# Fourier tables and the local mask of a fused attention and spectral-mixing kernel: loaded by SyncE, eight partitions at a time

## The chip, the cores and the metric

The kernel runs on one core of a Trainium2 chip. The metric is the device time of one execution in microseconds (us). A core has five engines that run their own instruction streams: TensorE (PE in the profile; its weight loads are PEld), VectorE (DVE), ScalarE (ACT), GpSimd (POOL) and SyncE (SP). They wait for each other through semaphores. Transfers between the device's memory (HBM) and the core's on-chip memory (SBUF, 128 partitions) are done by 16 DMA engines. An engine's instruction stream only issues a transfer; the transfer then runs on its own. In this kernel GpSimd issues the loads of inputs and weights, SyncE and ScalarE issue small loads of constants at the start and the stores of the output at the end.

## What is computed

The input is q, k and v with 8 batches, 8 heads, 576 positions and a head dimension of 64, and the spectral weights w_r and w_i (64 modes of 512 x 512) and w_ch (512 x 512), all float32.

```python
def _attn_ref(q, k, v):
    scores = scale * np.matmul(q, k.transpose(0, 1, 3, 2))
    rel = pos[:, None] - pos[None, :]
    mask_local = (rel >= 0) & (rel < stride)                 # stride = 32
    mask_strided = (rel >= 0) & (pos[None, :] % stride == pos[:, None] % stride)
    # heads 0-3 use mask_local, heads 4-7 mask_strided
    attn = softmax(np.where(masks, scores, -1e9))
    return np.matmul(attn, v)

def _moe_ref(x, w_r, w_i, w_ch):          # x: attention's output, (8, 576, 512)
    X = np.fft.rfft(x, axis=1)            # over the positions
    # the first 64 modes are multiplied by complex 512 x 512 weights, the others dropped
    Yr = einsum(Xr, w_r) - einsum(Xi, w_i)
    Yi = einsum(Xr, w_i) + einsum(Xi, w_r)
    y = np.fft.irfft(Y, n=S, axis=1)
    u = x + y
    return u + np.maximum(u @ w_ch, 0.0)
```

## The kernel before

The kernel has three stages. First comes the attention of heads 4 to 7 (strided mask), batch by batch, with a Fourier transform of each batch's result. Then comes the attention of heads 0 to 3 (local mask), again with the transform, and between its pieces the first half of the spectral products. Last come the second half of the spectral products, the inverse transform and the output. The transforms are products with tables of sines and cosines.

Seven constants are built on the host in float16 and loaded at the start. `cFs` (128 x 2 x 6 x 64) is the Fourier table for the strided heads, `cFl` (128 x 2 x 5 x 64) for the local heads, and `cA` (128 x 704) the table of the inverse transform. `cM6` and `cM5` are the strided masks, `cMl` (128 x 256) the local mask, and `cI` the identity matrix.

```python
names = ["cFl", "cFs", "cA", "cM6", "cM5", "cMl", "cI"]
...
def const_load(eng, *which):
    for n in which:
        eng.dma_start(cs[n][:, 0 : hosts[names.index(n)].shape[1]], drams[n])
...
load_str(0, 1)                                     # GpSimd: batch 0 of v, q, k
const_load(nc.scalar, "cI", "cM6", "cM5", "cFs")
load_str(1, 1)
const_load(nc.sync, "cMl", "cFl", "cA")
load_str(2, 2)                                     # GpSimd: batches 2 and 3
w_fetch()                                          # GpSimd: the first weight tile
```

The SBUF copies of `cFs` and `cFl` hold one more row than the host's: the negated sine part, which VectorE writes while the first batch is being prepared. It stands in VectorE's program between the copies of that batch's keys.

```python
first = str_front(0)         # 10 steps: transposes of v, q and k of batch 0, with copies
for i, w in enumerate(first):
    w()
    ...
    if i == 7:               # after the first of three steps on the keys
        for n in ("cFs", "cFl"):
            nc.vector.tensor_scalar(
                out=cs[n][:, 2], in0=cs[n][:, 0], scalar1=-1.0, scalar2=None,
                op0=AluOp.mult,
            )
```

`str_front(b)` transposes the inputs of batch b on TensorE (lines 269, 285 and 324) and copies the results with VectorE and ScalarE (lines 274, 292, 260 and 330). Then the loop over the batches runs, with `str_scores` (masks at line 345, scores at 353), `str_values` (line 374) and, a batch later, the transform `dft` (line 514). The inputs pass through a ring of four slots. A load into a slot waits until TensorE has transposed what was there.

```python
for b in range(B):
    if b in (1, 3):
        load_str(b + 3, 2)                         # two batches into slots of the ring
    load_loc(*[(), (), (), (), (0,), (1, 2), (3,), (4, 5)][b])
    w_fetch([2, 1, 1, 1, 1, 1, 0, 0][b])
    front = str_front(b + 1) if b + 1 < B else loc_front(0)
    for t in range(6):
        str_scores(b, t)
        ...                                        # values, transform, parts of front
```

In the second and third stage each weight tile (two modes) is loaded into one of five buffers (three more are borrowed in the first stage), used by the products of line 547 and then filled again. `w_fetch` issues these loads on GpSimd as two transfers, real and imaginary parts. GpSimd's stream is in order: a load that waits for a buffer holds back all later ones.

Of the kernel before, what the change touches and what calls it, by code (L numbers as in the profile page):

```python
# [29 lines left out]
def _host_consts():  # L30
    s = np.arange(S)
    m = np.arange(NM)
    ang = 2.0 * np.pi * np.outer(s, m) / S
    F2 = np.stack([np.sin(ang), np.cos(ang)], axis=1)


    Fl = np.zeros((128, 2, 5, NM))
    for t in range(5):
        Fl[: SCS[t], :, t] = F2[128 * t : 128 * t + SCS[t]]
    Fs = np.zeros((128, 2, 6, NM))  # L40
    for rp in range(2):
        for j, (a, z) in enumerate(JG):
            r2 = np.arange(a, z)
            ss = (32 * np.arange(NCB)[None, :] + 2 * r2[:, None] + rp).reshape(-1)
            Fs[: len(ss), :, 3 * rp + j] = F2[ss]

    A = np.zeros((4, 2, 16, S))
    for mm in range(NM):  # L50
        e = np.zeros(S // 2 + 1, dtype=np.complex128)
        for ri, unit in enumerate((1.0, 1j)):
            e[mm] = unit
            A[mm // 16, ri, mm % 16] = np.fft.irfft(e, n=S)
    A = A.reshape(2 * NM, S)
    A[:, :512] = A[:, :512].reshape(128, 256, 2).transpose(0, 2, 1).reshape(128, 512)
    none = np.zeros((128, 64))
    A = np.concatenate([A[:, :512], none, A[:, 512:], none], axis=1)

    ms = []  # L60
    for nr in (6, 5):
        n = nr * NCB
        kc, kr = np.arange(n) // nr, np.arange(n) % nr
        qr, qc = np.arange(n) // NCB, np.arange(n) % NCB
        ok = (kr[:, None] == qr[None, :]) & (kc[:, None] <= qc[None, :])
        blk = np.zeros((128, n))
        blk[:n] = np.where(ok, 0.0, NEG)
        ms.append(blk)

    rel = np.arange(160)[None, :] - np.arange(128)[:, None]  # L70
    blk = np.where((rel >= 0) & (rel < STRIDE), 0.0, NEG)
    last = np.full((128, 96), NEG)
    last[:64, 32:] = blk[:64, :64]
    ml = np.concatenate([blk, last], axis=1)
    f16 = [a.astype(np.float16) for a in (Fl, Fs, A, ms[0], ms[1], ml)]
    return f16 + [np.eye(128, dtype=np.float16)]
# [3 lines left out]
def kernel(  # L80
# [10 lines left out]
    nc = tc.nc  # L91
# [16 lines left out]
    def psum(kind, half=False):  # L108
# [4 lines left out]
    hosts = _host_consts()  # L113
    names = ["cFl", "cFs", "cA", "cM6", "cM5", "cMl", "cI"]
    drams = {
        n: nc.inline_tensor(np.ascontiguousarray(h), name=n).ap()
        for n, h in zip(names, hosts)
    }

    more = {"cFl": 1, "cFs": 1}  # L120
    cs = {
        n: consts.tile(
            [128, h.shape[1] + more.get(n, 0), *h.shape[2:]], F16, name=n + "_s"
        )
        for n, h in zip(names, hosts)
    }

    def const_load(eng, *which):
        for n in which:
            eng.dma_start(cs[n][:, 0 : hosts[names.index(n)].shape[1]], drams[n])  # L130

    idn = cs["cI"]

# [85 lines left out]
    def load_str(b, nb):  # L219
        for vi in (2, 0, 1):  # L220
            n = 3 * (b % 4) + SLOT[vi]
            two = ring[:, n : n + 4 : 3, :]
            src = SRC[vi][b - b % 2 : b - b % 2 + 2, 4:8].rearrange(
                "b h (c r) d -> (h c) b (r d)", r=32
            )
            if nb == 2:
                nc.gpsimd.dma_start(two[0:64], src[0:64])
            else:
                nc.gpsimd.dma_start(ring[0:64, n, :], src[0:64, b % 2])
            if b % 2 == 0:  # L230
                nc.gpsimd.dma_start(two[64:72], src[64:72])
# [465 lines left out]

    psum_pools(tp=3, sc=3, av=2)
    load_str(0, 1)
    const_load(nc.scalar, "cI", "cM6", "cM5", "cFs")  # L700
    load_str(1, 1)
    const_load(nc.sync, "cMl", "cFl", "cA")
    load_str(2, 2)
    w_fetch()

# [69 lines left out]
    for b in range(B):  # L775
# [12 lines left out]
        n = 0  # L788
        nm = NMODES[b]
        for mi in range(nm):  # L790
# [3 lines left out]
            n = upto  # L794
# [46 lines left out]
    n = 0  # L841
# [4 lines left out]
    for m in range(END):  # L846
# [7 lines left out]
        n = upto  # L854
# [165 lines left out]
```

The softmax here doesn't subtract the row's maximum and nothing guards it: scores larger than these inputs give would overflow.

## Time and profile before

The median of 3 runs is 433.9 us (433.64 to 435.1). The profiled execution has a span of 434.2 us.

| | busy, us | share of the span |
|---|---|---|
| TensorE, products | 338.5 | 78% |
| TensorE, weight loads | 244.5 | 56% |
| VectorE | 215.9 | 50% |
| ScalarE | 187.5 | 43% |
| GpSimd | 129.3 | 30% |

The page cuts the span into 40 equal slices of 10.9 us. A digit is the busy share of a slice in tenths, and the lines for DMA give the busy share of the 16 engines and the rate of what they moved. The queues are listed with the number of packets, the megabytes moved and the time of their packets as a share of 16 engines' span: q0 holds GpSimd's transfers, q1 SyncE's and q10 ScalarE's. The chain of waits follows the work that ended last back to what released it. In a timeline, a line has start, duration, engine, source line, operation and operands, and in brackets the idle time before it and what ended that.

The loads of the constants have these sizes and these times from issue to landing:

| constant | issued by | KB | issued at, us | us to landing |
|---|---|---|---|---|
| cI | ScalarE | 32 | 0.74 | 2.0 |
| cM6, cM5 | ScalarE | 27 and 22.5 | 1.14 and 1.6 | 2.6 and 5.8 |
| cFs | ScalarE | 192 | 2.10 | 6.6 |
| cMl | SyncE | 64 | 0.74 | 1.8 |
| cFl | SyncE | 160 | 1.14 | 2.5 |
| cA | SyncE | 176 | 1.60 | 5.5 |

### The profile page before, as it was taken

The numbers are of one execution on the slowest core, as the hardware profiler recorded it, in microseconds if no ns is written. First come the engines' busy times: TensorE is split into PE (matmuls) and PEld (weight loads), VectorE is DVE, ScalarE is ACT, GpSimd is POOL, SyncE is SP. The second block draws the span as 40 slices with busy tenths as digits, with TensorE's granted clock in tenths as the row PEclk, the third lists the DMA queues.
The fourth block names the chain that finished last, engine by engine and source line by source line (L and its number), as shares of the span: only waits on it lengthen the run. The fifth ranks groups of instructions, "written<-read, shape, count | busy, mean of one in ns | idle before, by whom it ended". The sixth has DMA issues, their size and how long they took to land.

```text
span 434.2 us, 12103 instructions
## 1 busy us (share of the span) xinstructions
PE 338.5 (78%) x5307; PEld 244.5 (56%) x5307; DVE 215.9 (50%) x468; ACT 187.5 (43%) x352; POOL 129.3 (30%) x208
## 2 busy tenths in 40 slices
PE   1986888779985787889885566587789798968993
PEld 1865776658864575667753344454456465643441
DVE  2888678744433243342511033355436366503894
ACT  1686678634643435444440401143215123602892
POOL 6433332322332222222222222222222221200992
PEclk9999899865985859875865569887958899988999
DMA  8999999999999999999999999999999999991787
GB/s 176 210 211 213 214 212 213 211 211 213 213 212 212 214 214 212 214 214 213 214 212 213 213 214 214 212 214 215 211 214 214 212 214 214 213 182 30 272 330 261
DMA packets 29140, 92.18 MB, mean 212 GB/s; under 512 B 4064, under 2 KB 5344, under 8 KB 29088
## 3 DMA queue, kind: packets, MB, share of 16 engines
q0 software_dynamic: 24704, 81.28, 94.4%
q1 hardware_dynamic: 3584, 9.59, 5.9%
q8 instruction: 42, 0.69, 0.6%
q10 hardware_dynamic: 800, 0.54, 0.5%
q14 instruction: 10, 0.08, 0.0%
HBM read 163.22 MB, written 9.44 MB: 398 GB/s over the span
## 4 chain that ended last, share of the span: by engine, by line
DMA 68%; PE 19%; DVE 6%; ACT 2%; issue 2%; POOL 1%; DVEq 0%; POOLq 0%
DMA wt<-in_moe_w_i_dram 51%; DMA wt<-in_moe_w_r_dram 11%; DMA ring<-in_q_dram 5%; PE y L547 2%; PE v L689 2%; DVE xb L250 2%; DVE kz L292 2%; PE u L689 2%; PE v L895 2%; PE sc L514 1%; ACT X L260 1%; PE tp L395 1%; DVE rec L249 1%; PE sc L441 1%; PE sc L353 1%
## 5 line engine op out<-in xcount | busy, mean ns | idle before, releaser
L547 PE MATMUL y<-X,wt 128*128 128x16 f16 (+1 forms) x2048 | 82.4, 192 | 61.0 <-DMA wt<-in_moe_w_i_dram 59.4
L547 PEld LDWEIGHTS <-wt 128*128 128x128 f16 (+1 forms) x2048 | 72.9, 103 | 76.5 <-issue 68.5
L196 POOL DMA_DIRECT2D wt<-in_moe_w_r_dram x62 | 36.5, 589 | 141.7 <-PE y L547 67.4
L196 POOL DMA_DIRECT2D wt<-in_moe_w_i_dram x60 | 35.4, 590 | 73.5 <-DMA wt<-in_moe_w_i_dram 61.2
L654 ACT ACTIVATE v<-sc 128x512 f16<-128x512 f32 x32 | 19.1, 597 | 69.7 <-PE sc L645 69.6
L645 PE MATMUL sc<-w_cp,xT 128*128 128x512 f16 (+1 forms) x160 | 48.2, 430 | 0.0
L471 ACT ACTIVATE PL<-sc 128x480 f16<-128x480 f32 (+1 forms) x48 | 27.3, 580 | 46.8 <-PE sc L457 46.5
L655 DVE COPY xo<-tp 128x512 f16<-128x512 f16 x32 | 22.1, 692 | 35.7 <-PE tp L653 35.6
L249 DVE RECIPROCAL rec<-av 90x4 f32<-90x4 f32 (+2 forms) x80 | 14.7, 184 | 46.2 <-PE av L486 34.8
L250 DVE TENSOR_TENSOR xb<-av,rec 90x256 f16<-90x256 f32 (+2 forms) x80 | 36.0, 450 | 2.7
L402 DVE COPY qT<-tp 128x576 f16<-128x576 f16 x16 | 12.0, 758 | 38.8 <-PE tp L395 35.9
L260 ACT ACTIVATE v<-tp 128x640 f16<-128x640 f16 (+1 forms) x24 | 19.4, 808 | 24.9 <-PE tp L429 22.1
L395 PE MATMUL tp<-cI_s,ring 64*64 64x64 f16 x864 | 26.7, 213 | 0.8 <-DVE qT L402 0.6
L360 ACT ACTIVATE PL<-sc 90x360 f16<-90x360 f32 (+1 forms) x48 | 22.7, 491 | 6.1 <-PE sc L353 5.3
L929 DVE TENSOR_TENSOR osb<-u,rl 128x512 f32<-128x512 f32 (+1 forms) x37 | 23.7, 674 | 1.8 <-PE u L689 1.1
L395 PEld LDWEIGHTS <-ring 64*64 64x64 f16 x864 | 21.1, 125 | 5.7 <-issue 2.6
L910 POOL TENSOR_TENSOR rl<-rl,xo 128x512 f32<-128x512 f32 x16 | 18.3, 1157 | 18.2 <-ACT rl L908 17.9
L441 PE MATMUL sc<-cMl_s,cI_s 128*128 128x480 f16 (+1 forms) x48 | 22.5, 468 | 1.6 <-ACT X L260 1.6
L457 PE MATMUL sc<-qT,kz 128*128 128x160 f16 (+1 forms) x160 | 22.4, 267 | 0.0
L908 ACT ACTIVATE rl<-v 128x512 f32<-128x512 f32 x36 | 20.4, 600 | 4.7 <-PE v L689 3.9
L285 PE MATMUL tp<-cI_s,ring 72*128 72x72 f16 x256 | 15.1, 206 | 9.4 <-DMA ring<-in_v_dram 7.9
L260 ACT ACTIVATE kz<-tp 64x360 f16<-64x360 f16 (+1 forms) x32 | 19.1, 595 | 7.7 <-PE tp L395 6.1
(103 smaller groups left out, 655.7 us busy)
## 6 DMA issues: line engine op xcount, KB each, us to landing
wt<-in_moe_w_r_dram POOLq DMA_DIRECT2D x62, 512.0 KB, 19.0
wt<-in_moe_w_i_dram POOLq DMA_DIRECT2D x60, 512.0 KB, 19.4
out_dram<-osb SPq DMA_DIRECT2D x14, 512.0 KB, 2.7
ring<-in_v_dram POOLq DMA_DIRECT2D x8, 288.0 KB, 13.3
ring<-in_q_dram POOLq DMA_DIRECT2D x8, 288.0 KB, 13.6
ring<-in_k_dram POOLq DMA_DIRECT2D x8, 288.0 KB, 13.5
ring<-in_v_dram POOLq DMA_DIRECT2D x3, 512.0 KB, 15.0
ring<-in_q_dram POOLq DMA_DIRECT2D x3, 512.0 KB, 14.8
```

Source lines behind the costliest of these rows:

```text
L196: nc.gpsimd.dma_start(dst, rows)
L250: nc.vector.tensor_tensor(out=dst, in0=val.rearrange("p h (q c) -> p h c q", c=4), in1=rec[0:n, 0:pieces] .to_broadcast((n, pieces, 64)) . ...
L260: nc.scalar.activation(out=out, in_=in_, func=ACTF.Copy)
L360: nc.scalar.activation(out=PS[0:n, ds(POFF[t], 4 * n)], in_=scp[0:n, 0 : 4 * n], func=ACTF.Exp, scale=SCALE,)
L395: nc.tensor.transpose(tp[ds(64 * hp, 64), ds(64 * i, 64)], qn[ds(64 * hp, 64), ds(64 * (9 * g + i), 64)], idn[ds(64 * hp, 64), ds(64 * hp, ...
L441: nc.tensor.matmul(scp[:, 0 : n * times].rearrange("p (h x) -> p h x", h=times), idn, mask_rows("cMl", n, times), start=True, stop=False,)
L457: nc.tensor.matmul(scp[:, ds(col, n)], kzs[par][:, hp, ds(s0, 128)], qTs[par][:, ds(s0, n)], start=False, stop=(i == len(todo) - 1),)
L471: nc.scalar.activation(out=dst, in_=src, func=ACTF.Exp, scale=SCALE)
L547: nc.tensor.matmul(yv[:, mi, e, :], wt[pr, XC[c], ds(128 * e, 128)], Xh[half][pr, c, :, :, m], start=(c == 0), stop=(c == 3),)
L645: nc.tensor.matmul(vp[pr, :], xT[:, ch, cols], w_chs["cp"][:, ch, :], start=(ch == 0), stop=(ch == 3),)
L655: nc.vector.tensor_copy(out=xo[pr].rearrange("p (h q c) -> p h q c", h=2, c=4), in_=tp[pr, 0:512].rearrange("p (h c q) -> p h q c", h=2, c=4),
L929: nc.vector.tensor_tensor(out=osb[:, t % 2, cols], in0=up[:, cols], in1=rls[b, t][:, t % 2, cols], op=AluOp.add,)
```

## The change

`const_load` gets a parameter for the number of partitions per transfer. The four larger constants, `cFs`, `cMl`, `cFl` and `cA`, are loaded by SyncE in 16 pieces of eight partitions each, in that order; before, `cFs` was loaded by ScalarE, and each constant was one transfer. The identity and the strided masks stay on ScalarE, as one transfer each. It is meant to take the large tables out of ScalarE's stream and to spread their traffic over a longer time, so that the first inputs meet less of it.

```diff
-    def const_load(eng, *which):
+    def const_load(eng, *which, rows=128):
         for n in which:
-            eng.dma_start(cs[n][:, 0 : hosts[names.index(n)].shape[1]], drams[n])
+            dst = cs[n][:, 0 : hosts[names.index(n)].shape[1]]
+            for p in range(0, 128, rows):
+                eng.dma_start(dst[ds(p, rows)], drams[n][ds(p, rows)])
...
     load_str(0, 1)
-    const_load(nc.scalar, "cI", "cM6", "cM5", "cFs")
+    const_load(nc.scalar, "cI", "cM6", "cM5")
     load_str(1, 1)
-    const_load(nc.sync, "cMl", "cFl", "cA")
+    const_load(nc.sync, "cFs", "cMl", "cFl", "cA", rows=8)
     load_str(2, 2)
     w_fetch()
```

## The prediction

> **What bounds the kernel now.** I read the slices of the page first, because they say whether one engine is busy everywhere, then the queues, then the chain of waits.
>
> ```profile
> DMA  8999999999999999999999999999999999991787
> GB/s 176 210 211 213 214 212 213 211 211 213 213 212 212 214 214 212 214 214 213 214 212 213 213 214 214 212 214 215 211 214 214 212 214 214 213 182 30 272 330 261
> q0 software_dynamic: 24704, 81.28, 94.4%
> q1 hardware_dynamic: 3584, 9.59, 5.9%
> q10 hardware_dynamic: 800, 0.54, 0.5%
> DMA 68%; PE 19%; DVE 6%; ACT 2%; issue 2%; POOL 1%; DVEq 0%; POOLq 0%
> ```
>
> The DMA engines run at one rate, about 213 GB/s, from the second slice to the thirty-fifth: the whole time in which GpSimd's loads (q0) pass. After that come 40 us of TensorE work and stores, which the change does not touch. So the kernel is a stream of 81.28 MB followed by a fixed tail, and the time changes by what lengthens the stream: a moment in which the DMA engines have nothing to do, or more work on the engine that finishes last. A 512 KB load takes 524288 / 213e3 = 2.46 us of that stream, a 288 KB load 1.38 us. Nothing that a transfer or an engine saves elsewhere counts.
>
> The second thing to look for is where compute decides when a load may be issued. That is in the timeline of GpSimd; columns are start, duration, instruction, and in brackets the idle time before it and its releaser.
>
> ```profile
> 21.63 0.59 POOL L196 DMA_DIRECT2D wt<-in_moe_w_i_dram  x1
> 24.45 0.58 POOL L227 DMA_DIRECT2D ring<-in_v_dram  x1 [2.23 <-PE tp L285]
> 27.36 0.58 POOL L227 DMA_DIRECT2D ring<-in_q_dram  x1 [1.78 <-PE av L374]
> 30.97 0.58 POOL L227 DMA_DIRECT2D ring<-in_k_dram  x1 [2.21 <-PE sc L353]
> ...
> 37.76 0.58 POOL L196 DMA_DIRECT2D wt<-in_moe_w_i_dram  x1 [1.86 <-DMA wt<-in_moe_w_i_dram]
> ...
> 101.15 0.59 POOL L196 DMA_DIRECT2D wt<-in_moe_w_i_dram  x1 [0.55 <-DMA ring<-in_k_dram]
> 105.90 0.58 POOL L196 DMA_DIRECT2D wt<-in_moe_w_r_dram  x1 [4.16 <-PE y L547]
> ```
>
> Where a load is not held by compute it is held by a load's landing, and the count fits the eighth load before it (the ninth load of all, at 5.99 us, was released by the landing of the first). So GpSimd keeps up to eight loads in flight, and that backlog hides a late issue up to its own length. I work the margins out at three places:
> - At 24.45 us. The load before it, issued at 21.63, is eight places ahead of the one at 37.76, so it landed at about 37.7. A new load needs at most the 1.8 us that the local mask takes from issue to landing in an empty queue. Margin 37.7 - 1.8 - 24.45 = 11.4 us.
> - At 58.49 us (a ring slot, released by a transpose) the same count gives about 69.1 - 1.8 - 58.5 = 8.8 us.
> - At 105.90 us (a weight buffer, released by mode products). The chain shows this load landing 10.82 us later, at 116.7; its own 2.46 us began at 114.3. Margin 114.3 - 1.8 - 105.9 = 6.6 us, the smallest I found.
>
> Third, the tables' own loads and their first reader, in the timeline of the first 16 us:
>
> ```profile
> 0.74 0.34 SPq L130 DMA_DIRECT2D cMl_s<-cMl  x1
> 1.14 0.42 SPq L130 DMA_DIRECT2D cFl_s<-cFl  x1
> 1.60 0.43 SPq L130 DMA_DIRECT2D cA_s<-cA  x1
> 2.10 0.45 ACTq L130 DMA_DIRECT2D cFs_s<-cFs  x1
> 14.47 0.26 DVE L741 TENSOR_SCALAR cFs_s<-cFs_s 128x384 f16<-128x384 f16 x1
> 14.65 0.36 DVE L741 TENSOR_SCALAR cFl_s<-cFl_s 128x320 f16<-128x320 f16 x1
> ```
>
> VectorE negates the sine part of both tables at 14.5 us, between copies that the attention of the first batch needs. Today the tables have long landed (the slowest, cFs, 6.6 us after its issue, at 8.7), so the two instructions wait for nothing.
>
> **What the Trainium skill says.** "DMA: Bandwidth & Descriptors", section "Why a DMA increments its semaphore by 16 and not by 1": a transfer runs on the largest number of engines up to 16 that divides its slowest dimension, on SyncE's kind of queue the lowest-numbered ones, so eight partitions would use 8 of the 16. No transfer of the kernel before has so few partitions from SyncE, so no run here shows it yet. The same page, "Queues, rings and completion order": each engine alternates between its queues packet by packet. The trace agrees in part: cA has eight rows for each of 16 engines and took 5.5 us under GpSimd's loads, where the local mask with as many rows took 1.8 us before they began. The same page, "Issuing engines are not separate DMA queues": a second issuer saves only its sequencer's time, so moving cFs from ScalarE to SyncE should bring nothing by itself; the trace has 0.45 us of ScalarE's queue for it. "TensorE: Matmul & The Clock Gate", section "What's actually happening": after an idle window of about 3.4 us the array runs at half clock until it has been busy as long. The trace agrees: the mask product of line 345 with 432 columns takes 0.55 us at 13.8 us and 0.35 us at 21.5 us.
>
> **The change part by part.**
>
> Removed: four issues (one on ScalarE's queue, three on SyncE's). ScalarE gets 0.45 us earlier to its table load at 2.6 us, but its first real work waits for TensorE until 8.8 us, so this is worth 0. In the first 9 us the loads of batch 0 share the engines with less table traffic (592 KB before); they may land about a microsecond sooner. But the bytes come later instead, and the stream is no shorter.
>
> Added: 4 x 16 = 64 issues on SyncE, in the order cFs, local mask, cFl, cA. SyncE's queue took 0.40 and 0.46 us from one start to the next. If the pace stays at 0.43 us, the last piece of cFs is issued at 0.74 + 15 x 0.43 = 7.2 us and landed well before 14.5 us. The last piece of cFl is the 48th: 0.74 + 47 x 0.43 = 20.9 us. It lands some 3 us later (1.8 us in an empty queue, plus its turn behind GpSimd's packets): 24 us. The 64th issue is at 27.8 us; cA's first reader is in the tail, and the local mask's is at about 91 us, so neither matters.
>
> If the pieces land slowly, the pace falls: if hardware-queue loads are also held to eight in flight, as GpSimd's are, a landing time of 4.5 us makes the pace 4.5 / 8 = 0.56 us, and cFl is complete at 0.74 + 47 x 0.56 + 4.5 = 31.6 us. I take a middle of 0.48 us and 4 us: 0.74 + 22.6 + 4 = 27.3 us.
>
> So VectorE stands still at cFl's negation from 14.65 us to about 27 us, 12.6 us (9 us at the quick end, 17 us at the slow end). VectorE runs its instructions in order and the copies of batch 0's keys come after, so TensorE and ScalarE stop within a microsecond or so. The attention that follows is bound by compute: from 43 to 106 us the chain has only engines. The one place where it can catch up is at 43.08 us, where TensorE waited 1.05 us for a load. TensorE's clock will be cold once more after the stall, but in the kernel before it was cold there as well (the array was slow until 19.7 us), so I add nothing. Delay of compute that arrives at 105.9 us: 12.6 - 1 = 11.6 us, say 11 (quick 8, slow 16).
>
> What becomes of it: the margins of 11.4 and 8.8 us swallow most, but at 105.9 us 11 - 6.6 = 4.4 us stay over, in which the DMA engines run dry (2 us of these at about 58 us already; the later place includes them). Quick 1.4 us, slow 9.4 us. After about 115 us, compute waits for weights and its delay is gone.
>
> Moved: the table traffic goes from 16 engines to 8. SyncE's queue spent 5.9% of 16 x 434.2 us on 3584 packets, 0.114 us each at 2.7 KB; for rows of 0.5 to 1.5 KB I estimate 0.06 us. Each of the eight has 64 rows where it had 32, 32 x 0.06 = 2 us more. A GpSimd load is complete only when its slowest engine is, so these 2 us count, but not beside an idle stretch of 2 us or more, which absorbs them. Sum: the larger of 2 us and 4.4 us, so about +4 us: 433.9 + 4.1 = 438 us.
>
> **The rivals.**
>
> (a) The margins hold everything. Pieces land in 2.5 us, the pace is 0.40 us, cFl is complete at 22 us, the delay of 7 us fits under the backlog. For it: every one of the issue durations is under 0.46 us, with 16 times the rows. Against: 6.6 us is a thin margin. Time: 434 to 436 us, of which the eight-engine imbalance is all.
>
> (b) The pieces crawl. A SyncE load has a completion packet for each engine beside its rows: 3584 is 3136 rows (1792 + 576 + 384 of stores, 384 of tables) plus 28 loads and stores x 16. If both of a piece's packets wait a turn behind GpSimd's packets of 0.3 us each (2.46 us over eight packets), the pace is 0.7 us, cFl is complete at 0.74 + 33 + 5 = 39 us, the delay is 23 us and the kernel takes about 17 us more: 451 us. For it: cM5's small rows landed only 5.8 us after issue. Against: cFs, queued behind it, came in just 1.3 us after it, nine packets an engine.
>
> (c) It gets faster, because batch 0's loads land first. They arrive sooner, but the negation stands in the path of the same batch, and the stream is full anyway: 433 us at best.
>
> **Range and chances.** The pace of the pieces carries nearly all the doubt: 0.40 us gives +1 to +2, 0.48 us +4, 0.56 us +9, 0.7 us +17. I give the first two together some 65%, the third 20%, the last 12%, a gain little. Faster by over 2% (under 425 us) needs a shorter stream, which no step offers: 0.02. Slower by over 2% (above 442.6 us) needs a delay of compute of 15 us or more: 0.23. Within 2%: 0.75. Eight times in ten: 434.3 to 446 us.
>
> **What would show it.** Right: 64 issues on SyncE 0.4 to 0.6 us apart, up to about 28 to 38 us; a wait on VectorE at line 741 for cFl of 9 to 17 us, with TensorE idle beside it; the load of 24.45 us issued some 10 us later; a slice of lower GB/s before 120 us, and none after; the tail as before, about 41 us. A SyncE queue of 3584 - 432 + 64 x (8 + 8) = 4176 packets shows eight engines at work per piece. Wrong: no wait at line 741 means the pieces are issued much faster than 0.4 us; a long wait without any dip in GB/s means the margins are larger than I reckon; a longer time without either means that it is the eight engines' share.

## The result, and the profile after

The changed kernel takes 448.7 us (median of 4 runs, 446.4 to 450.0) where the kernel before takes 433.9 us: a ratio of 1.033 (95% interval 1.029 to 1.037). It is 3% slower. The forecast of 438 us had the direction and not the size. The profile below is of the fastest of these executions, 446.4 us, with a span of 444.5 us, so it shows 12.5 of the 14.7 us.

The page of the changed kernel, the same lines as in the prediction:

```profile
DMA  8998999999589999999999999999999999993687
GB/s 145 215 218 170 209 210 212 210 211 203 99 152 214 213 213 213 214 213 214 214 212 213 213 214 213 214 214 213 214 213 214 213 214 213 214 212 67 260 318 274
q0 software_dynamic: 24704, 81.28, 92.6%
q1 hardware_dynamic: 4176, 9.78, 6.0%
q10 hardware_dynamic: 656, 0.35, 0.3%
DMA 62%; PE 22%; DVE 8%; ACT 3%; issue 2%; SPq 0%; POOL 0%; ACTq 0%; DVEq 0%
```

Read the rates first. The stream still runs at 213 GB/s, with two holes: the fourth slice (33 to 44 us, 170 GB/s) and the eleventh and twelfth (111 to 133 us, 99 and 152). The stream therefore ends one slice later. q1 has 4176 packets, as reckoned for pieces on eight engines (3584 - 432 + 64 x 16).

Who opened the first hole is in VectorE's waits up to 60 us; two of the lines (us in total, times, longest):

```profile
DVE cFl_s L743 <- DMA cFl_s<-cFl: 19.1, 1, 19.1
DVE cFs_s L743 <- DMA cMl_s<-cMl: 1.6, 1, 1.6
```

VectorE stands for 19.1 us at the negation of cFl. SyncE's timeline says why cFl is late; columns are start, time to the end of the last, and the count:

```profile
0.74 7.93 SPq L132 DMA_DIRECT2D cFs_s<-cFs  x16
8.72 11.46 SPq L132 DMA_DIRECT2D cMl_s<-cMl  x16
20.40 9.21 SPq L132 DMA_DIRECT2D cFl_s<-cFl  x16
29.79 9.25 SPq L132 DMA_DIRECT2D cA_s<-cA  x16
```

The first three tables take 29.05 us for 48 issues, 0.605 us each, although one issue occupies SyncE for only 0.26 to 0.29 us (medians of the four tables). The chain of waits up to 36 us shows what it waits for in between (start, duration, what; some lines left out):

```profile
1.60 4.37 DMA cM_s<-cM
5.98 0.26 SPq L132
...
8.39 6.31 DMA cFs_s<-cFs
14.71 5.19 DMA cMl_s<-cMl
19.92 4.38 DMA cMl_s<-cMl
24.32 5.01 DMA cFl_s<-cFl
29.34 4.75 DMA cFl_s<-cFl
34.12 0.05 issue
34.17 0.05 DVEq L743
34.22 0.05 issue
34.27 0.26 DVE cFl_s L743
```

Five landings of 4.4 to 6.3 us lie nose to tail. Each lets SyncE issue another piece, which in its turn takes about 5 us to land. With about eight pieces in flight that is 5 / 8 = 0.6 us a piece. The last piece of cFs landed only at 14.70 us (8.39 + 6.31), so even the negation of cFs waited a little. That of cFl starts at 34.27 us, where the kernel before had it at 14.65.

GpSimd's timeline of the changed kernel, at the places that correspond to those shown of before:

```profile
23.69 0.58 POOL L229 DMA_DIRECT2D ring<-in_v_dram  x1 [1.66 <-DMA ring<-in_k_dram]
24.26 0.57 POOL L233 DMA_DIRECT2D ring<-in_v_dram  x1
39.40 0.58 POOL L229 DMA_DIRECT2D ring<-in_q_dram  x1 [14.56 <-PE tp L271]
...
113.85 0.60 POOL L198 DMA_DIRECT2D wt<-in_moe_w_r_dram  x1 [11.68 <-PE y L549]
114.44 0.60 POOL L198 DMA_DIRECT2D wt<-in_moe_w_i_dram  x1
123.55 0.58 POOL L198 DMA_DIRECT2D wt<-in_moe_w_r_dram  x1 [8.50 <-PE av L488]
```

The load of v is not late: its slot had been freed before VectorE stopped. The load of q waits 14.56 us and is 12.0 us later than in the kernel before; the rate behind it falls to 115 GB/s (38 to 40 us).

The second hole has two dry stretches. The DMA engines moved nothing from 112 to 114 us, ahead of the load at 113.85 us, and nothing from 122 to 124 us, ahead of the one at 123.55 us. In the kernel before, the first of these two loads was held by a landing, not by compute:

```profile
100.00 0.60 POOL L196 DMA_DIRECT2D wt<-in_moe_w_r_dram  x1 [1.07 <-DMA ring<-in_q_dram]
```

The second is the one issued at 105.90 us before, now 17.65 us later. Of VectorE's 19.1 us, compute has made up 1.5.

### The profile page after: what moved, and what is told of

It reads as the page before. It is cut to its first block, busy times and chain, and to the rows that moved or that the text cites. A ratio compares the mean times of both kernels' runs of the same rounds, so it can differ in the third digit from the quotient of the medians.

```text
span 444.5 us, 12185 instructions
## 1 busy us (share of the span) xinstructions
PE 336.2 (76%) x5307; PEld 242.4 (55%) x5307; DVE 215.5 (48%) x468; ACT 187.4 (42%) x352; POOL 128.9 (29%) x208
## 3 DMA queue, kind: packets, MB, share of 16 engines
q1 hardware_dynamic: 4176, 9.78, 6.0%
## 4 chain that ended last, share of the span: by engine, by line
DMA 62%; PE 22%; DVE 8%; ACT 3%; issue 2%; SPq 0%; POOL 0%; ACTq 0%; DVEq 0%
DMA wt<-in_moe_w_i_dram 47%; DMA wt<-in_moe_w_r_dram 9%; PE y L549 4%; DVE kz L294 3%; DVE xb L252 2%; DMA cFl_s<-cFl 2%; DMA cMl_s<-cMl 2%; PE v L691 2%; PE u L691 2%; PE tp L397 2%; PE v L897 2%; DMA cFs_s<-cFs 1%; ACT X L262 1%; PE sc L516 1%; PE sc L443 1%
## 5 line engine op out<-in xcount | busy, mean ns | idle before, releaser
L647 PE MATMUL sc<-w_cp,xT 128*128 128x512 f16 (+1 forms) x160 | 49.9, 442 | 0.0
L656 ACT ACTIVATE v<-sc 128x512 f16<-128x512 f32 x32 | 19.1, 596 | 66.0 <-PE sc L647 65.8
L251 DVE RECIPROCAL rec<-av 90x4 f32<-90x4 f32 (+2 forms) x80 | 14.7, 183 | 38.0 <-PE av L488 27.5
L355 PE MATMUL sc<-qT,kz 128*128 128x90 f16 (+1 forms) x192 | 18.7, 217 | 18.4 <-DVE kz L294 17.9
L355 PEld LDWEIGHTS <-kz 128*128 128x128 f16 x192 | 15.0, 105 | 23.7 <-DVE kz L294 18.1
```

What stands on the lines that cost most here:

```text
L355: nc.tensor.matmul(scp[:, ds(n * h, n)], kz[:, rp, ds(72 * a + n * h, 128)], qT[:, ds(288 * h + a * NCB, n)], start=False, stop=(h == 3),)
L647: nc.tensor.matmul(vp[pr, :], xT[:, ch, cols], w_chs["cp"][:, ch, :], start=(ch == 0), stop=(ch == 3),)
```

## The experiments

Every ratio is against the kernel before, run on the same chip beside it; its median there was 433.9 us for the change and 434.5 to 435.3 us for the others. The waits are those of one traced execution, whose time is not the median: 446.4 us for the change, 442.7 for cFl second, 436.6 for 16 rows, 449.4 for the halves, 440.5 and 448.1 for the fills. The edits are against the changed kernel where nothing else is said.

| kernel | pieces | engines per piece | VectorE waits for cFl, us | us | ratio (95%) |
|---|---|---|---|---|---|
| the change | 64 | 8 | 19.1 | 448.7 | 1.033 (1.029 to 1.037) |
| negation late | 64 | 8 | none | 440.5 | 1.010 (1.006 to 1.014) |
| cFl second | 64 | 8 | 11.6 | 442.2 | 1.013 (1.011 to 1.016) |
| 16 rows | 32 | 16 | 8.0 | 435.8 | 1.001 (0.999 to 1.003) |
| whole tables | 4 | 16 | none | 434.8 | 0.999 (0.997 to 1.001) |
| halves | 64 | 16 | 20.5 | 447.1 | 1.026 (1.023 to 1.028) |
| halves, negation late | 64 | 16 | none | 435.1 | 1.000 (0.998 to 1.001) |
| four in flight, negation late | 112 | 8 | none | 447.5, one run | - |
| before, short fill | - | - | 15.3 (fill) | 441.1 | 1.016 (1.013 to 1.018) |
| before, long fill | - | - | 24.5 (fill) | 449.5 | 1.035 (1.033 to 1.037) |

**Negation late.** The pieces stay, the reader moves.

```diff
         if i == 7:
-            for n in ("cFs", "cFl"):
+            for n in ("cFs",):
                 nc.vector.tensor_scalar(...)
...
     for b in range(B):
+        if b == 4:
+            nc.vector.tensor_scalar(out=cs["cFl"][:, 2], in0=cs["cFl"][:, 0], ...)
```

> The changed kernel with one edit: cFl's sine part is negated by VectorE at the head of the fifth batch of the first stage instead of during the preparation of batch 0; cFs's negation stays. All 64 pieces are still issued by SyncE. Theory (the wait of VectorE for cFl, 19 us, is the whole loss): no wait at the negation, the rate of the DMA engines stays near 213 GB/s in every slice, 433.5 to 436.5 us, although the pieces land as slowly as before (last one of cFl at about 34 us). Rival (the pieces themselves slow GpSimd's loads, by their turns on eight of the engines): 440 us or more, with a lower rate and no wait.

It took 440.5 us. The wait is gone and most of the loss with it, but 5 us stay (95%: 2.7 to 6.1 us), and this is the rival's figure. So the pieces cost something by themselves. The rates of this kernel show where the rest is:

```profile
GB/s 141 215 218 217 213 210 188 202 193 211 213 211 214 213 214 213 214 213 215 212 212 214 213 214 213 214 213 213 215 212 215 212 216 211 215 201 39 266 327 275
```

There are no holes, but slices 7 to 9 (65 to 98 us) run at 188 to 202 GB/s, although the last piece was issued before 42 us. So the pieces do something to the stream that outlasts them. The packets' times in the kept traces show what. Each of GpSimd's loads ends with 16 completions. From the first to the last of them 5.4 us pass here (mean of the loads that land from 50 to 80 us), against 2.1 us in the kernel before. Some of the engines have fallen behind the others, and a load that needs them all lands late. In the changed kernel itself the figure is 3.1 us at 30 to 40 us and 1.9 us at 50 to 80 us: after the first hole the lag is gone.

**cFl second.** One word moves in the list:

```diff
-    const_load(nc.sync, "cFs", "cMl", "cFl", "cA", rows=8)
+    const_load(nc.sync, "cFs", "cFl", "cMl", "cA", rows=8)
```

> The changed kernel with another order: cFs, cFl, local mask, cA. The same 64 pieces; cFl's last one is the 32nd instead of the 48th. Theory (wait less the margins): at 0.6 us a piece the 32nd is issued at 0.74 + 31 x 0.6 = 19.3 us and lands 5 us later, at 24 us; the wait is about 9.5 us, the delay at the weight load of 105.9 us about 8 us, less the margin of 6.6 us: 435 to 437 us. Rival (cost per piece, whatever the order): 447 to 450 us. Rival (no margin, the wait adds in full): about 443 us.

The wait fell to 11.6 us and the time to 442.2 us. The order counts, so the loss is no constant per piece. But the theory's own sum gives 11.6 - 1.5 - 6.6 = 3.5 us for this wait, and 6.9 us came. The lag is in this trace too: 6.4 us from first to last completion at 50 to 80 us.

**Sixteen rows to a piece.**

```diff
-    const_load(nc.sync, "cFs", "cMl", "cFl", "cA", rows=8)
+    const_load(nc.sync, "cFs", "cMl", "cFl", "cA", rows=16)
```

> The changed kernel with pieces of 16 partitions instead of eight: 32 pieces, one row for each of 16 engines. If the pace is set per piece (two turns behind GpSimd's packets, or eight in flight with 5 us to landing), it stays at 0.6 us: cFl's last piece is the 24th, issued at 14.5 us, landed at 19.5 us, the wait 5 us, all of it inside the margins: 433.5 to 435.5 us. If the pace is set by bytes, a piece takes twice as long, cFl lands at about 34 us as before and the time is 447 to 450 us.

435.8 us: the loss is gone, just above what was expected. The view of DMA issues of this kernel has the reason (count, KB each, median us to landing):

```profile
cFs_s<-cFs SPq DMA_DIRECT2D x8, 24.0 KB, 4.6
cA_s<-cA SPq DMA_DIRECT2D x8, 22.0 KB, 6.4
cFl_s<-cFl SPq DMA_DIRECT2D x8, 20.0 KB, 5.9
cMl_s<-cMl SPq DMA_DIRECT2D x8, 8.0 KB, 5.6
```

A piece of 8 KB takes as long to land as one of 24 KB. The cost of a piece in this stretch is a time, not a number of bytes: half as many pieces, half the queue. VectorE waited 8.0 us, not 5, and that wait still vanished inside the margins.

**Whole tables, in the new order and from SyncE.**

```diff
-    const_load(nc.sync, "cFs", "cMl", "cFl", "cA", rows=8)
+    const_load(nc.sync, "cFs", "cMl", "cFl", "cA")
```

> The other part of the change alone: cFs moves from ScalarE to SyncE and the order is cFs, local mask, cFl, cA, but each is one transfer of 128 partitions. Theory: nothing waits, the tables are there by about 9 us, 433 to 435 us. Rival (the order or the issuer matters): a wait at the negation and more than 436 us.

434.8 us, no difference from before (0.999, 0.997 to 1.001). For whole tables neither the issuer nor the order matters; the cutting does.

**Halves: 64 pieces on 16 engines, with the early and the late negation.** A piece has 16 partitions and half of the columns.

```diff
-            dst = cs[n][:, 0 : hosts[names.index(n)].shape[1]]
+            w = hosts[names.index(n)].shape[1]
-            for p in range(0, 128, rows):
-                eng.dma_start(dst[ds(p, rows)], drams[n][ds(p, rows)])
+            for p in range(0, 128, rows):
+                for c in range(0, w, w // halves):
+                    part = ds(p, rows), ds(c, w // halves)
+                    eng.dma_start(cs[n][part], drams[n][part])
...
-    const_load(nc.sync, "cFs", "cMl", "cFl", "cA", rows=8)
+    const_load(nc.sync, "cFs", "cMl", "cFl", "cA", rows=16, halves=2)
```

> The changed kernel with pieces of 16 partitions and half of the columns: again 64 pieces, but each on all 16 engines, one row and one completion packet per engine and piece. So the eight lower engines have as many packets of pieces as in the changed kernel, and the upper eight as many as the lower. If the pace is set by turns of the pieces' packets it stays at about 0.6 us and VectorE waits about 19 us for cFl; that delay less the margin gives about +10 us, 443 to 447 us. If the loss needs the two halves of the engines to drift apart, 443 us or less is the part that is left; if all engines pay for the packets of the pieces, the 448 to 450 us of the changed kernel return.

> The same 64 pieces on 16 engines, and cFl's negation moved to the fifth batch, so that nothing waits. Against the kernel with 64 pieces on eight engines and the late negation (440.5 us, 5 us over the kernel before). Imbalance theory (the 5 us are the lag of the lower eight engines): 434.5 to 437 us, and no slices below 210 GB/s between 60 and 100 us. Rival (the 5 us are the turns that 64 pieces take, wherever they run): 439.5 to 442 us.

These two separate the parts. With the late negation the 64 pieces cost nothing (1.000, 0.998 to 1.001), against 1.010 for 64 pieces on eight engines: the 5 us belong to the eight engines and not to the number of pieces. From first to last completion of a load 1.7 us pass (50 to 80 us), and the rates have no weak slices between 60 and 100 us:

```profile
GB/s 145 212 214 216 216 213 211 211 211 213 213 212 215 213 214 213 213 214 214 214 212 212 213 213 215 214 214 213 213 214 213 214 213 213 215 205 47 268 333 275
```

With the early negation VectorE waits 20.5 us, the two holes are back, and the time is 447.1 us. That is the wait alone, +12 us in the median. The rates and the wait of that kernel:

```profile
GB/s 145 212 214 153 204 196 209 212 212 211 116 125 213 213 214 213 214 212 215 213 215 212 213 215 213 214 214 212 214 214 213 214 214 213 213 213 64 259 325 262
DVE cFl_s L745 <- DMA cFl_s<-cFl: 20.5, 1, 20.5
```

The instructions on cA in the same kernel end with the line of its landing times (least, median, most):

```profile
DMA to landing us min/median/max: 1.6/4.4/5.1
```

Part of cA is loaded while GpSimd's stream has run dry; a piece then lands in as little as 1.6 us. The 5 us are those of a piece behind GpSimd's stream.

**Four in flight.** With the late negation, cA's pieces are loaded in groups of four, each group four times; a piece that is written again waits for its own landing.

```diff
-            for p in range(0, 128, rows):
-                eng.dma_start(dst[ds(p, rows)], drams[n][ds(p, rows)])
+            for p in range(0, 128, rows * group):
+                for _ in range(times):
+                    for i in range(p, min(128, p + rows * group), rows):
+                        eng.dma_start(dst[ds(i, rows)], drams[n][ds(i, rows)])
...
-    const_load(nc.sync, "cFs", "cMl", "cFl", "cA", rows=8)
+    const_load(nc.sync, "cFs", "cMl", "cFl", rows=8)
+    const_load(nc.sync, "cA", rows=8, group=4, times=4)
```

> Late negation, pieces of eight partitions; cA's pieces are loaded in groups of four, each group four times over, 64 issues in all, and a piece that is loaded again must wait until it has landed: about four in flight instead of eight. Theory (the pace is set by the turns of a piece's two packets behind GpSimd's packets on each engine): cA's issues stay about 0.6 to 0.7 us apart and a piece lands in about 2.7 us. Rival (landing takes 5 us whatever is in flight, and eight in flight then make 0.6 us): 1.2 us apart, 75 us or more for the 64 issues.

SyncE's timeline of this kernel:

```profile
21.70 10.40 SPq L134 DMA_DIRECT2D cFl_s<-cFl  x16
32.14 80.83 SPq L134 DMA_DIRECT2D cA_s<-cA  x64
```

cFl's pieces are 0.65 us apart, cA's 80.83 / 64 = 1.26 us. My theory of turns had 0.6 to 0.7 and falls; the rival's figure is met. Four times 1.26 is 5.0 us: a piece takes 5 us to land whether four or eight are under way, and the number in flight turns that into a pace. Nothing waits for cFl, and yet the one execution took 447.5 us. The 48 pieces more are 0.54 MB, an estimated 2.5 us at 213 GB/s. The rest fits a lag that grows with them: from 100 to 130 us the completions of a load come in two groups of eight, on average 4.8 us apart (0.1 us in the kernel before, at 50 to 80 us).

**Fills, on the kernel before.** No transfer is changed; VectorE is kept busy with fills of a buffer that is written again before it is read.

```diff
         if i == 7:
+            for _ in range(7):        # 11 in the long one
+                nc.vector.memset(Xh[1], 0.0)
             for n in ("cFs", "cFl"):
```

> The kernel before, tables untouched, with seven fills of a buffer added on VectorE ahead of the negation (the buffer is written again before it is read): no transfer is added, only about 12.5 us in which VectorE is taken from the first batch. Theory (a delay of compute less the margin of 6.6 us and about 1.5 us that is caught up): about +4 us, 438 to 441 us, and a dip of the rate near 110 us. Rival (the whole delay is hidden, and what the changed kernel lost came with the pieces' traffic): 434 to 436.5 us. Rival (no margin): 447 us.

> The same with eleven fills, about 19.5 us, as long as VectorE's wait in the changed kernel. Theory: 19.5 - 1.5 - 6.6 = about +11 us, 444 to 448 us, as with 64 pieces on 16 engines (447.1 us), and the difference to seven fills is the difference of the fills, 7 us. Rival (traffic matters too): 442 us or less, or more than 450 us.

The fills held VectorE longer than I had reckoned, because each waited for the one before. VectorE's timeline of the short fill:

```profile
26.03 1.76 DVE L741 MEMSET X<- 128x2048 uint32 x1 [0.49 <-DVE X L741]
28.29 1.76 DVE L741 MEMSET X<- 128x2048 uint32 x1 [0.49 <-DVE X L741]
29.97 0.20 DVE L743 TENSOR_SCALAR cFs_s<-cFs_s 128x384 f16<-128x384 f16 x1
30.09 0.23 DVE L743 TENSOR_SCALAR cFl_s<-cFl_s 128x320 f16<-128x320 f16 x1
30.35 1.09 DVE L292 COPY kz<-tp 64x360 f16<-64x360 f16 x2
```

The last of these, the copy, in the kernel before and with the long fill:

```profile
15.02 1.07 DVE L292 COPY kz<-tp 64x360 f16<-64x360 f16 x2
39.50 1.09 DVE L292 COPY kz<-tp 64x360 f16<-64x360 f16 x2
```

The delays are 15.3 us with seven fills and 24.5 us with eleven. Both times lie above what was expected (438 to 441 and 444 to 448 us). Set against the loss of the same traced execution, the fills' 15.3 us cost 6.0 us and their 24.5 us cost 13.6 us; the halves' 20.5 us cost 14.2 us and the change's 19.1 us cost 12.5 us. Hidden are 9.3, 10.9, 6.3 and 6.6 us. A late first batch with no table traffic at all thus loses most of what the halves lose. Why the fills hide some 3 to 4 us more is open.

## Why the prediction was wrong

The forecast was +4 us; +14.7 us came.

**What bounds the kernel, and how a delay gets through: right.** A stream at one rate, holes where compute holds back a load, the tail no longer than it was. The margin of 6.6 us at the weight load of 105.90 us and the 1 us caught up made 7.6 us hidden; the four traced executions above have 6.3 to 10.9. With the wait that occurred the sum gives 19.1 - 1.5 - 6.6 = 11.0 us, and the traced execution lost 12.5. The second hole is near 110 us, as foretold, but it opens at the load that had stood at 100.00 us, which I had not reckoned. The place of the first was off: not the load of v but that of q came late.

**Step "the pieces' landing": the term that failed.** I took 4 us to landing and 0.48 us a piece for the middle, cFl complete at 27.3 us and a wait of 12.6 us. Measured: about 5 us, 0.605 us, the negation at 34.3 us, a wait of 19.1 us; even cFs, which I had landed well before 14.5 us, came at 14.7. Because the landing time enters 47 times through the pace (an eighth of it each time) and the margin is taken off afterwards, one microsecond of landing is worth nearly 7 us of wait, and what exceeds the margin reaches the end. I had the formula, pace = landing / 8, and read the landing wrong: the tables' landings of 5.5 to 6.6 us stood in the profile before, and I had read them as the time of eight rows an engine. The four-in-flight run and the 16-row run show that, for these pieces, size and number hardly enter; cM5 with 22.5 KB took 5.8 us too. Rival (b) had the direction, and its mechanism, a pace set by packets taking turns on the engine, is what the four-in-flight run speaks against. Why a piece takes 5 us behind GpSimd's stream stays open.

**Step "from 16 engines to 8": too small, but right that an idle stretch absorbs it.** I put 2 us, hidden beside the idle stretch. Where nothing waits, eight-engine pieces cost 5 us (440.5 against 435.3 us), and the same number of pieces on all 16 engines costs nothing. The completions show the lag of some engines behind the others, 5.4 us from first to last; in the four-in-flight run they part into eight and eight. How this lag becomes 5 us of time is not shown. Beside the long wait no such cost shows: the lag is gone after the first hole, and the traced execution of the change hid as much of its wait as the halves on 16 engines (6.6 and 6.3 us). The median of 448.7 us is 2.3 us above that execution; the slower ones have no trace, so what they lose besides is open.

**Steps on ScalarE's 0.45 us, on the order and on the early start of batch 0: right.** Batch 0's first transpose of q started at 9.02 us instead of 10.19. Whole tables from SyncE in the new order are no different from before. Nothing was gained by spreading the traffic. None of the kernels tried is measurably faster than the kernel before; the changed one loses its loss with pieces of 16 rows.

## What to carry to other kernels

Count small transfers as time, not as bytes: behind this stream, which filled the DMA engines, each piece of 4 to 24 KB took about 5 us to land, and the number in flight divided that into a pace. Then find the first reader of the last piece and ask whose instruction stream it blocks; moving one instruction to a later place took away two thirds of this loss. Look also at how many engines a small transfer uses: here 64 pieces on eight of them put those behind, and the large loads across all 16 ended with the slowest.

## What the runs showed of the hardware

- Under GpSimd's loads, a SyncE transfer of 8 to 24 KB landed in 4.6 to 6.4 us (medians of four tables, pieces of 16 rows), with no order by size; in the run with halves, with the stream dry, the least was 1.6 us.
- With about four of them in flight instead of eight the spacing went from 0.65 to 1.26 us, so the landing time stayed at about 5 us.
- Eight-partition transfers use eight engines, as the Trainium skill has it ("DMA: Bandwidth & Descriptors", section "Why a DMA increments its semaphore by 16 and not by 1"): 4176 packets on SyncE's queue fit 8 rows and 8 completions a piece.
- 64 such transfers of 4 to 12 KB, with nothing waiting for them, cost 1.0% (0.6 to 1.4%); as many on 16 engines cost 0.0% (-0.2 to 0.1%).
- With them on eight engines, the 16 completions of one GpSimd load lay 5.4 us apart from first to last, against 2.1 us in the kernel before and 1.7 us with the pieces on 16 engines (loads that land from 50 to 80 us).
